# The row maxima of a group: turned by TensorE in float32 and scaled by VectorE, in place of a 16-bit copy and a DMA transpose

## The chip, the cores and the metric

The kernel runs on one core of a Trainium2 chip. The core has TensorE (PE in the profile, its weight loads PEld), VectorE (DVE), ScalarE (ACT), GpSimd (POOL), and SyncE (SP), which here only issues DMAs. Each works through its own queue in the order in which the program stands, and waits on semaphores for the others. Matrix products land in PSUM (8 banks of 2 KB per partition), all else lives in SBUF. The metric is the device time of one execution in microseconds (us); lower is better.

## What is computed

Attention over 8 batches, 12 heads, 448 rows and 64 columns, whose output goes through a layer of 8 experts of 448 tokens each:

```python
q_n, k_n = rmsnorm(q, g_q), rmsnorm(k, g_k)
scores = scale * np.matmul(q_n, k_n.transpose(0, 1, 3, 2))
scores = scores - np.max(scores, axis=-1, keepdims=True)
attn = np.exp(scores)
attn = attn / (np.sum(attn, axis=-1, keepdims=True) + 1e-09)
x = np.matmul(attn, v)            # then [B, H, S, D] -> [B*S, H*D]
logits = x @ w_gate               # pairs in falling order, 448 tokens per expert
out[mask_e] = np.maximum(x[mask_e] @ w1[e], 0) @ w2[e]
```

The change lies in the subtraction of `np.max`. The maximum of a row of scores sits in one partition, while the kernel computes the scores transposed, so it must be carried over to the free axis, as one row of 448 numbers per head.

## The kernel before

**Two stages.** Attention runs from the start to about 430 us, the router and the experts from there to the end. The change lies in the first. Attention works in 24 groups of 4 heads (`g` = 0 to 23); groups 0 and 1 (`EARLY`) have a path of their own, without the transposes below, and 22 groups take the common one.

**One group.** q and k are loaded (`load_qk`, L239 and L231) and normalised (ACT L289, L301, L303, L327; DVE L295; POOL L306 to L309, L330, L359), split into a high and a low half in 16 bits (`hi`, ACT L368; `lo`, POOL L371) and turned by two DMA transposes on SP's queue, `trh` for the high halves and `trl` for the low ones (`transpose`, L380, kq<-s). Then:

- `max_score` (PE L501) multiplies the high halves into a PSUM tile pm, seven blocks to a group; `max_reduce` (DVE L510) takes the maxima of a block into two columns of mx. The pool of pm has one buffer, so a block's products wait until the maxima of the block before are taken.
- `put_max` (ACT L519) scales the 14 columns of maxima into a 16-bit tile qm, `tr_max` (SP L430) turns qm into mt by a DMA transpose of 128x128, and `row_max` (SP L436) moves the 14 rows of mt by a DMA into rowq, whose two rows hold the maxima of the group.
- `scores` (PE L532, 12 products, and L534, 4 products with rowq, which subtract the maximum) fills psc; `exp` (ACT L540) makes e; `split` (POOL L556) makes the low half pl; `av` (PE L582, and L588 to L592) multiplies with v into po; DVE normalises and splits po (L632 to L652) into xa.
- After six pairs of heads a batch is done: SP stores xa (L667, L670) and turns it by four DMA transposes for the gate (`xtr`, L659).

**What sets the order.** `plan` lists every piece of work with its engine, what it needs and which buffers it uses; a table of numbers, `ORDER`, names the sequence in which all pieces are written out, and thereby the order on every engine's queue. Nothing is reordered when the program runs: an instruction that waits holds up all that stand behind it on its engine. On SP, a `tr_max` or `row_max` that waits holds up loads, stores and the transposes of q and k. Buffers: kq 3, s1 2, pm 1, psc 2, po 2, pl 5. `early` (DVE L1183 to L1223) is the router's work on the first 21 columns of logits; it stands among the last groups of attention.

Of the kernel before, what the change touches and what calls it, by code (L numbers as in the profile page):

```python
# [89 lines left out]
class Attention:  # L90
# [420 lines left out]

    def put_max(self, g, a=None):
        scale = 0.125 / (self.QS * self.KS)
        o, i = (t[:, :14].rearrange("p (h b) -> p h b", h=2) for t in (self.qm[g % 2], self.T["mx", g]))
        some = [(slice(0, 128), slice(0, 7))]
        if a is not None:
            some = [(slice(0, 128), slice(4 * a, 3 + 4 * a)), (slice(64 * a, 64 * a + 64), slice(3, 4))]
        for r, b in some:
# [429 lines left out]
    def plan_first(self, plan, g, a):
# [51 lines left out]
        "Cq2FHv3QHwHx3RCvCw2H2I2e3o3n493T3S3U3V373W4dOJCxCy2JOOOROI2f2g3pHy2hH-Cz4AC+3qHz4BI03rOHOMOLOKONC-I24CD0U92i2j"  # L1000
        "3EI3H+3sI13tI4I53uD1OUOSUAD2UBD3D438392n3F3GUC3vI7OQD5D6UD4DI6I84e4E3w3y3AOPOTD7D8UEUFI9IBIAD9UGDAUHOV2kOWOZDB"
        "OdOYObOaDCUIDDDEIC4gOcOXOeUJUKDFULDG4fOhOfOi4F3z3x4G0B4H3B3CDHDIIDIE4I3+3-IGOk3XIH51DJ5Q5S3Y5U5RUMUNDKIJOgDLDM"
        "IMIKIO4JIN4hIP4L4iDNDOOj3a4jUOUPIQDPDQUQURIS3d3ZOlOmDRDSUS3DIFIIIL4MOoOsOtOpOqOr3b53IRIT4k4mDTDUIUOnUTOu4K4l3c"
        "4N3e3f5V5TDVIV52DW404146OwIXDX54DYO+Oz4nIWIY4o4q4r0CIaIbDZDaIdOv55Ie56DbUUUVDcUWIfIhDdDeUXIgIiIjIkOyDfOxO-P0Dg"
        "UYUZUa5759DhDi4p4O42484s4t586I6K47IlIoImIZIc5AInIpDjIr43UbDk4P4Q5W5Y5BIsDlDmUcUh6JUfIu4RP7P3P2Dn5XDoP8P1PEP6P4"
        "P5IqIv5D5E5Z5aDpUrDqIwIxUsUtP9DrDs5b44455v5xUu5w6LIyIzI+Uk5FI-5c5eDtDuUvPAPBPDPCUwDvDwJ3J0Dx5yUxDyUyJ14uJ4PFPG"
        "ItPH5C5d5z5g5+4SUzU+5fJ25hPNPKPIPLPMPJU-6NDzV0D+J6J9J7JA5iD-E0V1POPPE1E2V2JBJCJD4TUiUj4vE3E4JFPQE5PT5G4V4W6M4w"
        "JEJG0qE66O6PV3PUPSPR5j5-61E7E8V4V5JHJI4X5k5l4+V6JKE9EAV7V8UlUmUnJL607AJ5J8634U6264JJJM6QUoUpJQEBJN5HJO7BUe504-"
        "5I7FUd7CUg5JEC6RJR6nPVEDEEUqPcPaPZPYPbPdEFEGPePfPXEJEK656p6S660D0E6T6UJS4xJT4yPWV9VAEHEIJUJVJW67ELVBVCEMVD6oPj"
        "PiPkPhPgJX6WPlPm4zJPPnEN6V6YVE0FVFVG6X6ZVHEO5K5L5m5N5O7D7E5P5nVIVNVP5oVQ68PtPsPoPqPpPrEPEQJYJbJZJcVXJaJd6a6bER"  # L1010
        "Pu6qESJeJh6rJfETEUPvJjEVP+VYVZVaEWVb7GJiJk6sJlJn6c7I6t6uJmJoEXEY7H6vPzPxPwPyVcVdEZEaJpJqJsEbP-Q0Jg0G0H5MQ10I0J"
        "6x7JEc69VeVfJvJtJw6wJr7K7L6zEdEeVgQ5Q3Q7Q4Q2Q6VhViEfEgVjVkVlJyJ+EhVOVRVTVSEiVU5p5qJzJ-VV7f7hQ8QDEjEk7gK2K0ElVW"
        "Em5s5u82838786VM6A6dVJ5t846B6-QBQAQEQ9QCEnQF7MJu6+7OK17iEoJx5r0K6y7NK3QH7j7k7l7PQG6C6D6EEpK4K5K6K7K8K9Eq6F6G6H"
        "VK856k6m7Q6e6f706lVL6gErVmVnVoEsVpQKQLQJKAKB7S7T0LEtEu0M7RQIQNQMVrKCKD7mExVsVqEyVtKFQOQPEvVuEwKEKG88Vv8A7n7oKJ"
        "KH7U7V8w8x8+Ez8B89E+KIKK8C8X8D8ZQUQSQRQTQQQVVwE-VxVyF0VzQYQdQaQZQbQcF1F2V+7172W3W5W4KLKOF3F4QWQXWDWE8aQeQkF5F6"
        "KM8E0NKP7pKR6h7rKSQgQhF7F8KUKW6i7377W679KVKXFBWFFCWGWHQjKNKQ7s6j7qKT8F0OKYF9Ka7t7u8GKZ0P0Q8HFAQiQfWIWJKb748YQl"
        "QmQnQoQqFDWKFEWLKcKd758I8b8cKf8JFFWMFGQpQtQrW7QsWNWOWPKi7WKgKj8yFHFIWQWRW9W8Kl8KKmKnFJKoFKWAQuQy90WB8z8-FLFMW2"
        "7X787cW07d7YKrKp8MKe8d8LKh8NFP91WCFQ9293KqKsQ+QxQvQwQ-QzWSFNWTFOKtKwFR76KkR6R7R5R4R3R28f8e9oW19s9r9pKuKv94957Z"
        "968gKx7a9P9R7bWUFSWVWWFTFU7v7wV-9q7e9t7xKz0RKyK+8h8j8kL0L1FVFWR8RDRBFXFYR1R0REK-WXWYFZFaL2L6FbWZFcWaWbL398R9RC"
        "L47-8l8081FdRAFeL5L7RFRGRH8i97RIRMRJRNWcWdWeWfWgWlFfFgL87yL9LB7zLCFhFi9Q8O0S999A9uWn8U8P8mWi9SRORQRPLEFjFkLFLH"  # L1020
        "RLRKWvFlFmLJRUFnWwWxFo9w9TLILK9CLLLNLMLOFpWyWzFqRTRSRRRVRWW+FrW-X0FsX1LA7+9B0T0ULDLGRcRdRaRbRY9D9U9VFtFuX28Q9E"
        "9FWo9X9WAgLPLSFvRXReRgFw9vLQLRLTLU8n8o8VWmAh8pFxLVFy8R8S8TLWRZX3LY9ZFz9x9y9zF+X4X5LaLZLb0V9YAHAJ9bRjRiF-G0X6Lc"
        "LdLeG1G2X7LfRfAlWk8WRkRh8q8rX8G3WpWqWrX9G4XAXBXCLjG5LgLhWsWtLkG6WuAKAIRlLXRtRpRqRsRrRoG7RuRvRmRnG89dAiG9XDXEGA"
        "XFLmRz9c9a9+8s9-0WLiLlA0Ln9GAmA18tWhGBGCLpLqLrLsALAMA2A4Aj8uWjAk9M9N8vAoGFAnGGXGXHRxRyRwR+GDXIGEXJLtLv9O9H9e9I"
# [1031 lines left out]
```

## Time and profile before

| | us |
|---|---|
| three runs | 929.72, 933.79, 932.5 |
| their median | 932.5 |
| the profiled execution | 933.5 |
| its span in the profile | 931.7 |
| attention, up to the last normalised pair | about 431 |
| router and experts | about 500 |

The profile lists busy time by engine and stretch, the granted clock of TensorE as a share of its full speed (1.00 is 2.4 GHz), what an engine waited for, and a chain of work followed back from the last instruction. A busy PE is not PE at its peak, since the ends of its matmuls are modelled. For SP the rows give the time that issuing a DMA took; the transfer itself lands later.

### The profile page before, as it was taken

The page shows a single profiled execution, that of the slowest core. Times are in us where ns is not written, and L with a number is a line of the kernel's source. Part 1 is how long each engine was busy: PE and PEld are TensorE (multiplying, and loading weights), DVE is VectorE, ACT ScalarE, POOL GpSimd, SP SyncE. Part 2 cuts the span into 40 slices and gives each one's busy share as a digit, 9 for nine tenths or more (in the row PEclk, how much of TensorE's full clock was granted, in tenths as well). Part 3 has the DMA queues.
Part 4 walks back from the last instruction along what each step waited for, and adds up shares of the span by engine and source line. Part 5 has one row for each costly group of instructions (what it writes and reads, how often), then busy time and mean ns, then how long its engine had stood idle before and what let it go on. Part 6 is the DMA issues. An engine that isn't in the chain of part 4 may idle for free.

```text
span 931.7 us, 29734 instructions
## 1 busy us (share of the span) xinstructions
PE 858.7 (92%) x12783; PEld 566.5 (61%) x12784; DVE 681.9 (73%) x1483; ACT 522.0 (56%) x954; POOL 443.2 (48%) x470
## 2 busy tenths in 40 slices
PE   2799998898999899976799999999999999999996
PEld 1476766665677667756456556565565555655873
DVE  7899988786898689676787777776867758239630
ACT  6999998796989788642142434243333424234421
POOL 7899999886989879882101103021112020120101
PEclk9999999998999899998699999999999999999999
DMA  6689999899999987831454829492937749481401
GB/s 178 155 169 177 182 201 197 207 186 208 206 183 197 189 173 138 168 88 62 150 183 148 276 91 270 141 302 98 301 122 234 198 164 292 150 143 44 152 19 43
DMA packets 262009, 158.02 MB, mean 170 GB/s; under 512 B 183028, under 2 KB 248564, under 8 KB 261876
## 3 DMA queue, kind: packets, MB, share of 16 engines
q1 hardware_dynamic: 256434, 133.63, 61.9%
q0 software_dynamic: 4608, 22.02, 7.0%
q8 instruction: 100, 1.64, 0.8%
q10 hardware_dynamic: 834, 0.46, 0.2%
q14 instruction: 33, 0.27, 0.1%
HBM read 94.40 MB, written 22.02 MB: 125 GB/s over the span
## 4 chain that ended last, share of the span: by engine, by line
issue 37%; PE 24%; POOL 13%; ACT 8%; DVE 8%; DMA 7%; SPq 2%; POOLq 0%; ACTq 0%; DVEq 0%
PE ph L1833 6%; DMA kq<-s 5%; PE psc L532 4%; POOL pl L556 3%; PE py L1850 3%; ACT qn L327 3%; ACT e L540 3%; PE po L582 3%; POOL out_dram L1866 3%; POOL rows L1770 3%; DVE mx L510 2%; PE pm L501 2%; POOL s L371 2%; DVE st L295 1%; PE psc L534 1%
## 5 line engine op out<-in xcount | busy, mean ns | idle before, releaser
L510 DVE TENSOR_REDUCE mx<-pm 128x2 f32<-128x896 f32 x162 | 176.3, 1088 | 55.3 <-PE pm L501 52.8
L1833 PE MATMUL ph<-xt,w1h 128*128 128x448 f16 (+2 forms) x708 | 183.5, 343 | 0.4 <-DVE xt L1791 0.3
L1866 POOL DMA_INDIRECT out_dram<-y,idx x32 | 34.1, 1067 | 307.5 <-ACT y L1852 238.2
L540 ACT ACTIVATE e<-psc 128x896 f32<-128x896 f32 x168 | 147.3, 910 | 34.9 <-PE psc L534 34.5
L556 POOL TENSOR_TENSOR pl<-e 128x896 f16<-128x896 f32 x84 | 140.5, 1688 | 18.9 <-ACT e L540 15.3
L532 PE MATMUL psc<-kq 64*64 64x448 f16 x2016 | 130.0, 360 | 4.6 <-ACT e L540 2.4
L1850 PE MATMUL py<-w2h,hh 128*128 128x384 f16 x384 | 125.0, 326 | 0.0
L1850 PE MATMUL py<-w2h,hl 128*128 128x384 f16 x384 | 125.0, 326 | 0.0
L1850 PE MATMUL py<-w2l,hh 128*128 128x384 f16 x384 | 125.0, 326 | 0.0
L1833 PE MATMUL ph<-xt,w1l 128*128 128x448 f16 (+2 forms) x354 | 119.9, 343 | 0.0
L582 PEld LDWEIGHTS po<-v,e 128*64 128x64 f32 x2940 | 94.0, 139 | 22.0 <-issue 20.7
L582 PE MATMUL po<-v,e 128*64 128x65 f32 x2940 | 105.4, 225 | 1.4 <-issue 0.9
L1850 PEld LDWEIGHTS <-hh 128*128 128x128 f16 x768 | 73.6, 97 | 45.6
L1822 ACT ACTIVATE hh<-ph 128x448 f16<-128x448 f32 x56 | 30.4, 543 | 125.0 <-PE ph L1833 121.9
L1833 PEld LDWEIGHTS <-w1h 128*128 128x128 f16 x708 | 64.8, 97 | 52.6 <-issue 1.5
L1852 ACT ACTIVATE y<-py 128x384 f32<-128x384 f32 x48 | 23.5, 489 | 116.1 <-PE py L1850 95.6
L1770 POOL DMA_INDIRECT rows<-xd,idx x32 | 31.5, 983 | 115.2 <-DVE idx L1540 46.8
L501 PE MATMUL pm<-kq 64*64 64x448 f16 x648 | 63.7, 378 | 23.0 <-DMA kq<-s 13.7
L532 PEld LDWEIGHTS <-kq 64*64 64x64 f16 x2016 | 60.8, 109 | 36.3 <-issue 12.3
L327 ACT ACTIVATE qn<-qkraw,st 128x64 f32<-128x64 f32 x308 | 75.8, 340 | 3.3 <-POOL st L309 2.3
L588 PE MATMUL po<-vs,e 128*128 128x65 f16 (+1 forms) x696 | 65.0, 197 | 3.5 <-DVE z L632 3.5
L1637 DVE SCALAR_TENSOR_TENSOR w2l<-stage,w2h 128x768 f16<-128x768 f32 x64 | 60.2, 951 | 8.9 <-ACT w2h L1633 8.8
(293 smaller groups left out, 1887.9 us busy)
## 6 DMA issues: line engine op xcount, KB each, us to landing
stage<-in_moe_w_dram SPq DMA_DIRECT2D x64, 768.0 KB
vraw<-in_v_dram SPq DMA_DIRECT2D x24, 384.0 KB
xd<-xa SPq DMA_DIRECT2D x16, 576.0 KB
qkraw<-in_q_dram SPq DMA_DIRECT2D x11, 768.0 KB
qkraw<-in_k_dram SPq DMA_DIRECT2D x11, 768.0 KB
vraw<-in_v_dram SPq DMA_DIRECT2D x48, 32.0 KB
xd<-xa SPq DMA_DIRECT2D x16, 96.0 KB
qkraw<-in_q_dram SPq DMA_DIRECT2D x22, 64.0 KB
```

Of the source, the lines that this page charges most:

```text
L327: self.nc.scalar.activation(o[:, h, b], x[:, h, b], AF.Copy, scale=self.T["st", g][:, 1, 14 * i + n:14 * i + n + 1])
L501: self.nc.tensor.matmul(o, q[r, mine], k[r, all_], start=True, stop=True)
L510: self.nc.vector.tensor_reduce(m, p[r, :, :448], axis=AX.X, op=OP.max)
L532: mm(o, k[r, mine], q[r, all_], start=i == 0, stop=False)
L540: self.nc.scalar.activation(e, p[:, :, :448], AF.Exp, scale=scale)
L556: eng.tensor_tensor(l, self.T["e", d], self.T["ph", d], op=OP.subtract)
L582: nc.tensor.matmul(out, self.T["e", d][:, h, q0:q0 + m], self.v32[g % 2][:, h, slot], start=begin, stop=end)
L588: nc.tensor.matmul(out, e[:, h, q0:q0 + m], vh, start=begin, stop=False)
L1637: self.later(0.93, lambda w=w: self.nc.vector.scalar_tensor_tensor(l[:, w], v[:, w], self.WS, h[:, w], op0=OP.mult, op1=OP.subtract), k, i)
L1833: nc.tensor.matmul(p, a, b[:, o], start=st, stop=sp)
L1850: nc.tensor.matmul(p, a[:, f, s], b[:, f, o], start=st, stop=sp)
L1866: st = nc.gpsimd.indirect_dma_start(out=self.out, out_offset=bass.IndirectOffsetOnAxis(ap=self.router.idx[k][:n, c:c + 1], axis=0), in_=y[ ...
```

## The change

For the 22 groups of the common path the maxima stay in float32. mx is now two fixed tiles of 128x64 (14 columns used, the rest set to zero once). `turn_max` on PE multiplies each half of mx (64 partitions) with a 64x64 unit matrix in float32 into a tile of the ring pm, which turns it; `top_max` on DVE reads 14 rows of 128 from PSUM, scales them and writes the 16-bit mt of 14x128; `row_max` on SP moves mt as before. `put_max` remains for groups 0 and 1 alone. The unit matrix is written once by ACT. `tr_max` is gone: SP issues 276 DMAs in attention and not 298. ORDER is a new table.

```diff
-        self.qm = tiles(2, [128, 128], F16, "qm")
+        self.qm = tiles(2, [128, 14], F16, "qm")
+        self.mx = tiles(2, [128, 64], F32, "mx")
+        self.unit = c.tile([128, 64], F32, name="unit")
...
-    def tr_max(self, g):
-        t = self.T["mt", g] = self.w.tile([128, 1, 128], F16, name="mt", bufs=self.RINGS["mt"])
-        self.nc.sync.dma_start_transpose(t, self.qm[g % 2])
+    def units_of(self):
+        for r in (slice(0, 64), slice(64, 128)):
+            self.nc.scalar.activation(self.unit[r], self.router.ident[r, r], AF.Copy)
+
+    def turn_max(self, g):
+        p = self.T["tm", g] = self.ps.tile([128, 2, 512], F32, name="pm", bufs=self.RINGS["pm"])
+        for n, r in enumerate((slice(0, 64), slice(64, 128))):
+            self.nc.tensor.matmul(p[:64, n, :64], self.mx[g % 2][r], self.unit[r], start=True, stop=True)
+
+    def top_max(self, g):
+        t = self.T["mt", g] = self.w.tile([14, 128], F16, name="mt", bufs=self.RINGS["mt"])
+        i, scale = self.T.pop(("tm", g))[:14, :, :64], 0.125 / (self.QS * self.KS)
+        self.nc.vector.tensor_scalar(t.rearrange("p (n c) -> p n c", n=2), i, -1.0 / self.ROW,
+                                     math.log(self.PSC) / (scale * self.ROW), op0=OP.mult, op1=OP.add)
...
-        self.nc.sync.dma_start(q[0:128:64].rearrange("p (b c) -> p b c", c=128), t[:14, 0])
+        self.nc.sync.dma_start(q[0:128:64].rearrange("p (b c) -> p b c", c=128), t)
...
-                add("put", "A", US["small"], self.put_max, g, after=[("mx", g), ("c", "qm")], make=("top", g),
-                    opens=[("qm", g)], uses=[("mx", g)])
-                add("trm", "S", US["trm"], self.tr_max, g, after=[("top", g)], make=("mt", g), opens=[("mt", g)],
-                    uses=[("qm", g)], move=(1.5, 0.25))
+                add("tmx", "T", 0.11, self.turn_max, g, after=[("mx", g), "unit"], make=("top", g), uses=[("mx", g)],
+                    holds=[("pm", ("tm", g))], modes=[3] * 2)
+                add("cmx", "D", 0.27, self.top_max, g, after=[("top", g)], make=("mt", g), opens=[("mt", g)],
+                    frees=[("tm", g)])
...
+        add("unit", "A", 0.45, self.units_of, after=[("rc", 2)], make="unit")
...
     ORDER = (
-        "00030507040m0u0x0w08090v0n0106020o100+0z0y0-1113121P141Q15161RZs1719181A1S1T1U1C1t1w1s1u1z1x1v1-2L2o2q2s1E1B1V"
+        "0u0m0407050v0w0x08090y0z0n0+0-03020601000oZs11131P12141Q1516171RZt1S181T1U1V1s1x1u1v1t1z1+1A0A101O0B191C1B1D1E
...
```

Three places show how the queues change; line numbers of the changed kernel are 2 to 13 higher.

SP around the maxima of group 11 and the transposes of q and k of group 13 (rows of kq<-s; xt<-xa are the transposes of a finished batch), before:

```order
L430 DMA_TRANSPOSE mt<-qm_131 128x1x128
L659 DMA_TRANSPOSE xt<-xa 128x12x128 x3
L436 DMA rowq_129<-mt 2x7x128
L277 DMA vraw_132<-in_v_dram 128x4x192
L659 DMA_TRANSPOSE xt<-xa 128x6x128
L231 DMA vraw_132<-in_v_dram 64x2x64
L380 DMA_TRANSPOSE kq<-s_4629 128x14x128 x2
```

and now:

```order
L667 DMA_TRANSPOSE xt<-xa 128x12x128 x2
L449 DMA rowq_129<-mt 2x7x128
L667 DMA_TRANSPOSE xt<-xa 128x12x128
L382 DMA_TRANSPOSE kq<-s_4686 128x14x128
L233 DMA qkraw<-in_k_dram 64x4x64
L667 DMA_TRANSPOSE xt<-xa 128x6x128
```

The transpose of qm is gone, two transposes of the batch and not three stand ahead of the DMA into rowq, and the first transpose of group 13 stands behind one more of the batch and ahead of the fourth, where it stood behind all four and two loads of v.

DVE around the last maxima of group 11 (L510 and L521 take maxima; L295 and L297 are sums of squares of a later group; L442 is `top_max`; mx_4157 and mx_1_133 are group 11's, mx_4566 and mx_0_132 group 12's), before:

```order
L510 TENSOR_REDUCE mx_4157<-pm_4450 128x2
L648 CAST xa_3359<-po_4293 128x7x64
L510 TENSOR_REDUCE mx_4157<-pm_4513 128x2
L652 TENSOR_TENSOR xa_3359<-po_4293,xa_3359 128x7x64
L510 TENSOR_REDUCE mx_4566<-pm_4561 128x2
```

and now:

```order
L521 TENSOR_REDUCE mx_1_133<-pm_4488 128x2
L297 TENSOR_REDUCE st_4218<-sq_1_140 128x14
L442 TENSOR_SCALAR mt_4568<-pm_4565 14x128
L660 TENSOR_TENSOR xa_3423<-po_4249,xa_3423 128x7x64
L521 TENSOR_REDUCE mx_0_132<-pm_4597 128x2
```

Between the last maxima of one group and the first of the next DVE now empties the turned maxima, here behind a sum of squares; on PE one block of scores stands between `turn_max` and the next products into pm.

DVE near the end of attention, with the end of `early` before (L1223) and its first row now (L1192); L760 and L768 empty the gate's products of batch 6, z and po belong to pair 44; before:

```order
L1191 TENSOR_SCALAR keyi_105<-keyi_105 128x21
L1192 CAST key_106<-keyi_105 128x21
L1193 TENSOR_SCALAR key_106<-keyi_105 128x21
L1223 TENSOR_TENSOR cmp_107<-key_106,hit0_80 128x672
L760 TENSOR_TENSOR logits_63<-po_9675,lsc_9822 128x24
L761 TENSOR_TENSOR logits_63<-po_9675,lsc_9822 64x8
L632 TENSOR_SCALAR z_9839<-po_9688 128x7
```

and now:

```order
L768 TENSOR_TENSOR logits<-po,lsc 128x24
L769 TENSOR_TENSOR logits<-po,lsc 64x8
L640 TENSOR_SCALAR z<-po 128x7
L644 TENSOR_TENSOR po<-po,z 128x7x64
L656 CAST xa<-po 128x7x64
L660 TENSOR_TENSOR xa<-po,xa 128x7x64
L1192 TENSOR_REDUCE best<-logits 128x21
```

`early` now stands behind the gate of batch 6 and behind the pair of heads 44, where it stood ahead of both.

## Rows read from the trace of the kernel before

**Rows 1.** Busy time by stretch: us and instructions of each engine, granted clock, DMA share.

```profile
core 0: us, PE busy (x) PEld busy (x) DVE busy (x) ACT busy (x) POOL busy (x), PEclk, DMA share, GB/s
50.00:125.00 75.00, 72.76 (x1713) 53.08 (x1712) 69.51 (x99) 74.18 (x163) 72.34 (x67) 1.00 0.95 172
125.00:375.00 250.00, 230.03 (x5622) 168.54 (x5615) 202.46 (x302) 212.32 (x448) 216.05 (x205) 0.97 0.95 188
...
200.00:225.00 25.00, 20.68 (x461) 13.87 (x456) 16.53 (x26) 18.05 (x36) 23.09 (x22) 0.87 1.01 194
...
432.00:931.00 499.00, 479.87 (x3889) 291.37 (x3889) 332.72 (x958) 166.66 (x210) 69.10 (x104) 0.97 0.57 167
```

**Rows 2.** Chain that ended last, shares of 50 to 432 us by line.

```profile
by line: DMA kq<-s 11.9%; PE psc L532 8.7%; POOL pl L556 7.4%; PE po L582 6.4%; issue 6.3%; ACT qn L327 5.8%; ACT e L540 5.8%; PE pm L501 4.8%; DVE mx L510 3.8%; POOL s L371 3.8%; PE psc L534 2.9%; PE po L588 2.5%; SPq L659 2.2%; POOL qn L3
```

**Rows 3.** Pieces of that chain: start us, us, what.

```profile
93.16 5.86 DMA kq<-s
...
213.95 5.54 DMA kq<-s
...
365.17 6.34 DMA kq<-s
```

**Rows 4.** Timeline of SP: start us, us, line, DMA, tiles, count.

```profile
213.25 0.65 SPq L231 DMA_DIRECT2D vraw<-in_v_dram  x1
213.95 5.09 SPq L380 DMA_TRANSPOSE kq<-s  x2
...
359.41 5.66 SPq L659 DMA_TRANSPOSE xt<-xa  x3
365.17 2.52 SPq L380 DMA_TRANSPOSE kq<-s  x1
```

**Rows 5.** DMA issues by tile: ns min/median/max, first and last start in us.

```profile
L430 SPq DMA_TRANSPOSE mt<-qm x22: 1122/1201/1780, 60.0 to 399.4; - x22
L436 SPq DMA_DIRECT2D rowq<-mt x22: 550/582/803, 64.3 to 401.7; - x22
...
L380 SPq DMA_TRANSPOSE kq<-s x44: 1380/1982/4541, 35.7 to 387.6; - x44
```

**Rows 6.** Who waited for whom: us in total, times, longest.

```profile
SPq L436 <- DMA mt<-qm: 11.0, 12, 3.0
...
PE pm L501 <- DMA kq<-s: 13.7, 9, 4.1
PE pm L501 <- DVE mx L510: 6.6, 7, 3.8
PE psc L534 <- DMA rowq<-mt: 1.5, 4, 0.7
```

**Rows 7.** Groups by form up to 425 us: count, busy us, mean ns, idle before.

```profile
L510 DVE TENSOR_REDUCE mx<-pm 128x2 f32<-128x896 f32 x162 | 176.3, 1088 | 55.3 <-PE pm L501 52.8 <-ACT v L477 1.3
...
L582 PE MATMUL po<-v,e 128*64 128x65 f32 x2940 | 105.4, 225 | 1.4 <-issue 0.9 <-DVE xa L652 0.5
...
L295 DVE TENSOR_REDUCE st<-sq 128x14 f32<-128x910 f32 x44 | 47.7, 1090 | 0.9 <-ACT sq L289 0.8
...
L648 DVE CAST xa<-po 128x448 f16<-128x448 f32 x47 | 29.0, 618 | 0.6
...
L632 DVE TENSOR_SCALAR z<-po 128x7 f32<-128x7 f32 x47 | 7.4, 158 | 11.0 <-PE po L592 9.4 <-PE po L582 1.3
...
L519 ACT ACTIVATE qm<-mx 128x14 f16<-128x14 f32 x22 | 4.6, 208 | 0.4 <-DVE mx L510 0.3
```

**Rows 8.** Timeline of DVE near the end of attention.

```profile
402.21 0.32 DVE L1183 TENSOR_REDUCE best<-logits 128x21 f32<-128x168 f32 x1
...
411.25 0.17 DVE L760 TENSOR_TENSOR logits<-po,lsc 128x24 f32<-128x24 f32 x1
```

**Rows 9.** Timeline of ACT and POOL there; idle time before in brackets.

```profile
415.49 1.73 ACT L540 ACTIVATE e<-psc 128x896 f32<-128x896 f32 x2 [6.32 <-PE psc L534]
...
422.49 3.32 POOL L556 TENSOR_TENSOR pl<-e 128x896 f16<-128x896 f32 x2 [0.98 <-PE po L592]
```

More of the change, by code (lines that the diff above doesn't have):

```diff
@@ L163, in maxima @@
         def maxima():
-            for t in self.qm:
+            for t in self.mx:
                 nc.gpsimd.memset(t, 0.0)
@@ L190, in __init__ @@
         D, G = nc.vector, nc.gpsimd
-        self.later = [("P", 0.3, eps, "eps"), ("P", 0.3, maxima, "qm"), ("P", 0.4, rowk, "rowk")]
+        self.later = [("P", 0.3, eps, "eps"), ("P", 0.3, maxima, "mx"), ("P", 0.4, rowk, "rowk")]
         self.later += [("P", 0.47, lambda t=t: zero(t), ("rowq", i)) for i, t in enumerate(self.rowq)]
@@ L505, in max_reduce, with put_max @@
         g, b = divmod(n, 7)
-        if ("mx", g) not in self.T:
-            self.T["mx", g] = self.w.tile([128, 14], F32, name="mx")
         r = slice(0, 128) if some is None else slice(64 * some, 64 * some + 64)
-        m = self.T["mx", g].rearrange("p (h b) -> p h b", h=2)[r, :, b]
+        m = self.mx[g % 2][:, :14].rearrange("p (h b) -> p h b", h=2)[r, :, b]
         self.nc.vector.tensor_reduce(m, p[r, :, :448], axis=AX.X, op=OP.max)
-    def put_max(self, g, a=None):
+    def put_max(self, g, a):
         scale = 0.125 / (self.QS * self.KS)
[L514 to L518, printed above, removed]
+        o, i = (t[:, :14].rearrange("p (h b) -> p h b", h=2) for t in (self.qm[g], self.mx[g]))
+        for r, b in ((slice(0, 128), slice(4 * a, 3 + 4 * a)), (slice(64 * a, 64 * a + 64), slice(3, 4))):
             self.nc.scalar.activation(o[r, :, b], i[r, :, b], AF.Copy, scale=-1.0 / self.ROW,
@@ L865, in plan @@
                 first = n % 7 == 0
-                add("red", "D", US["reduce"], self.max_reduce, n, some, after=[("pm", n, some)], make=("mx", *x),
+                add("red", "D", US["reduce"], self.max_reduce, n, some, after=[("pm", n, some), ("c", "mx")], make=("mx", *x),
                     opens=[("mx", g)] if first else (), uses=() if first else [("mx", g)], frees=[("m", n, some)])
@@ L986, in plan_first @@
                      frees=[("tf", i, *x)])
-        part("put", "A", 2 * small, self.put_max, *x, after=[("mx", *x), ("c", "qm")], make=("top", *x), opens=[("qm", g)],
+        part("put", "A", 2 * small, self.put_max, *x, after=[("mx", *x)], make=("top", *x), opens=[("qm", g)],
              uses=[("mx", g)], port=False)
@@ L1000 @@
[L1000 to L1024, printed above, removed]
@@ new lines @@
+        "2w2U2T2W3H2x2y2z1d2ACPCQ3J1K2BCVCWCXCYCbCZCaCc1L2Y2CCd292X2+301M1NHh2V272-321iHi3134HkHlCeCj1j2D3K3I2a3L1k3M1p"
+        "3g3h3l1q3j1r3i3k3mCk1lCfCgHnHoCh2ZCi2EHq2FHrCnCo2bClCmOFCrCsHs36CtCuOGHuCpCq2c33353N3PHtHw37CvCw3nHj1oHmHpOHOK"
+        "ONOMCx2GHv3oHx2HOLOJOI3O4Y4Z2l2m2e3R2d3Q493T4d3VCy2fOOOROT2I2J3pU92h2g3q2i3r2j3S3U2n3E4c4a3W3G4b3sCzHyHz4AUAC+"
+        "H-I04BC-UBD0I2D1I3UCD24CI5OSD3D4OUI7D5D6OQOPUE3uI6I83839UDUFD7D8UGIBI9D9DAUHOV2kH+3tI1I43vOXOZ4D3w4E3BDBOdOaOY"
+        "ObOcDCUIDD3y4F3zIAICOWOe4e4H3F3A3+4g3x4G5Q3-4I0CDEOjDFOhOi4fDGDHUJUKDIULIDIGIEIH51DJDKUMOfIJ3X3Y5V3Z5UIKIM4JIN"
@@ new lines @@
+        "IFII3C3d3eIL3DDLUNDMOkIOIPDN52DOOgUO4hISDPDQUPUQIQOlOmDR4L4N5T5R4M3a4iIR4jIT3b53OqOsOtOoOrDSDTURDUUS4k4mIUIVIX"
+        "DVDWOpOuOzDX544K3c4l4o554nDYOxOwOnUT4041UUUVIaIY56IbIW57DZDa4qOyIdDbUWDcIfOvIeIg5S4O425WDdUXDeIhIjDf0DDgIiIk4r"
+        "IZIc59O+O-P0Dh5XDiUYUZ460p483f47IlIoDjP5P7P4P3P6P2P14p4s4tImIpUaDkUbUcDlDmIrIu434PUrUs4Q444V4WUh4RIs4XUkUtP8Dn"
+        "DoPEIwDp5Y5Z585v5B5A5D45InIqIvIx5a5bDqPBPDPADr5wDsUuIyIzI+5xI-5F6I6J6N0E5E5c5eDtDuP9PCDvUvDwUwUxJ0J1J3J4DxDyPF"
+        "PGItPH4uUy0F4vUzPKPJPLPIPM5C5d5g5y5zDzD+J6J75+5fJ2J50G5-J9JAD-U+E0PNJBJCE1E2U-V0V1JDJFE3E4POPPPTE50q5i5j4SJEJG"
@@ new lines @@
+        "4T4U61V2E6V3PRPUPQE7E8PSUi5G4wUj4xV4V5V65kUlUmUnE9EAV7JHJIJKEBJLUoJNEC5HV8JQ5IED6L6K6M6OEEPV0H0I5h5l60JOJRUpUq"
+        "634yJ86264JJUe4+7A7C4-Ug5J7E6P6Q6nJSEFEG6RPcPYPdPaPZPbPXJTPWEJEKV96o6S6T656UJUJV6pJWJX66JM4zJP6VEHPePgPhPiVAEI"
+        "VBELPkPfPjVCEMVDENVEEOVFVGJYJb7B67Uf507DEP6W6XJZEQPlJeJc5mVH5nVIJh5KERESPmPuPnET6qEU5LJf6YJi6a7GPpPsPoPtPqPrUd"
+        "VXEVVYEWJjJlJkJmEXEYVZPyJnEZ68VaVbEa7FVNVQVJ5oVP6cVO5N5PVL5s5O5u5tJaJd0J5MJgP+PxPwPzP-Q0PvQ16r6s6tJo7I6b6Z6u0K"
+        "0L6vEbJpJq7JJsJt7H7K7LQ7Q2Q3Q5VcVdVeEcVf696AVg82856B8387Jv6wJw7fEdQ6Q4EeJyEfVhViVjEgVkJ+JzJ-6x6z7hVRVSVTEhEiVl"
@@ new lines @@
+        "HKYaNCNDNENFBSHNHOYETFTGHLBRNGNJY5NHNIHMHPTKYDTMTLTITJTNHQHRHSNKYFBTYGNPNMNNNQCFHTTHTOTRTUTSYbHUYcYdYeTPTQTTNL"
+        "BUBuYfYgYhBvYiYjYkBWBxByBtY4Y6B+B-C0BwYpYsYoYrYqYnYlNSNTNVHVHWNWNONRCECGTVTbTZTXTaTWTYNYHXHYNbHbHcNZNcNhNeHZYz"
+        "Y+HaY-Z0NUNXNaNfNiTcTgTdThTeTiTfCKZ5Z6HdNkHeZ1Z7HfNlNnNoHgZ8NqNrCHNtCICJNuCLYmZ9YtBzNdNgNjNmTjTpTlTnTkToTmZEYv"
+        "YuYwYxZFYyNzNwNxNpNsNvCMTqTsTvTrTwTuTtZMZGZHZIZrZNZOZPZQN+NyN-O0O1O3O6O2O4O7O5O9OAOCODZ2O8TxTyT-TzU1U0T+OBZAZC"
+        "Z3ZRZTZSOEZVZWZXZYZZU2U4U6U3U7U8U5ZdZeZfZgZhZiZlZ4ZJZKZUZBZDZaZnZbZcZpZoZLZqZmZkZj"
```

38 lines of the change are left out of this document (22 added, 16 removed).

## The prediction

> **What bounds the kernel now.** The busy times by stretch come first, since a sum over the whole span mixes two programs. From 432 us on TensorE is busy 479.87 of 499 us and nothing in that stretch is touched [rows 1]. So a gain of attention moves the end one for one, and the question is what attention waits for. From 50 to 125 us ACT is busy 74.18 of 75 us and POOL 72.34: two engines are full. From 125 to 375 us no engine is: ACT 212.32, POOL 216.05, PE 230.03 of 250, and the granted clock falls to 0.97 [rows 1]. Something that is not an engine holds that stretch up. If it ran as densely as the one before, POOL would need 216.05 x 75 / 72.34 = 224 us of it, ACT 212.32 x 75 / 74.18 = 215 us. So 250 - 224 = 26 us is the most that freeing the hold-up can give.
>
> The chain of waits names it: its largest share in attention is the landing of kq<-s, 11.9% of 382 us, 45 us [rows 2], in nine pieces between 93.16 and 365.17 us [rows 3]. What a piece waited for is to be read on SP's own timeline: the transposes at 213.95 us start 0.05 us after the load before them was issued, and those at 365.17 us 0.10 us after three transposes of xa that took 5.66 us [rows 4]. They were not late for want of data just made; they stood in SP's queue. The transposes of q and k are what PE waits for: 13.7 us directly, against 1.5 us for the row of maxima itself [rows 6]. So the row is hardly late; it is the place that the maxima take on SP that counts.
>
> **The change part by part.** The sum is made on the profiled execution, 933.5 us (span 931.7).
>
> *SP loses 22 transposes.* One costs SP 1.20 us of issuing in the median [rows 5], and the DMA behind it waits for its landing 11.0 us in all, 0.5 us per group, with every load and transpose behind it [rows 6]. That is 1.7 us per group, or 37 us of SP's time. What reaches the end is what the nine pieces give: two come as a pair, so eight times 1.7 = 13.6 us if each is issued that much earlier. The table adds to it at the two places that I looked up: group 13's transpose no longer stands behind a fourth transpose of the batch and two loads, and in the row shown [rows 4] the three transposes ahead of the piece at 365.17 us are no longer ahead of it. Against it, POOL and ACT are the next to be late. Bounds: 0, if SP fills the slots with longer issues of what remains, and -26, POOL's limit above. I take -10, three quarters of the eight, since the stretches between the pieces are led by ACT, POOL and PE already.
>
> On this a page of the Trainium skill speaks otherwise. Here a transpose costs SP 1.20 to 1.98 us in the median and up to 4.54, the plain DMA into rowq 0.58 [rows 5]. "Advanced Engine Details and Errata", section X-Bar Transpose, states that transposes are as fast as ordinary DMAs on trn2. By that rule a slot would be worth 0.58 + 0.5 us and the term about -6; the rows speak against it, and the sum goes by the rows.
>
> *The clock.* A full clock in the 250 us, where it is 0.97 [rows 1], would be worth up to 7.5 us of PE's time, and the one stretch shown at 0.87 is one in which PE was busy 20.68 of 25 us only [rows 1]. I give back a fifth of that, -1.5 (0 to -7.5).
>
> *ACT loses 22 copies* of 0.208 us, 4.6 us [rows 7]. ACT leads at least 11.6% of the chain [rows 2]: -0.5 (0 to -4.6).
>
> *DVE gains 22 instructions* of 14x128 from PSUM; the 14 partitions don't matter if the time goes by elements per partition. Between 128x7 at 158 ns and 128x448 at 618 ns [rows 7] that is 158 + 121 x 1.04 = 284 ns, 6.2 us in all. DVE leads about 4% of the chain by the one line shown [rows 2]; I double it for the lines not shown: +0.4 (0 to +6.2).
>
> *PE gains 44 float32 products* of 64x64. The nearest row is L582, float32 with 65 columns: 105.4 us for 2940, 36 ns each packed, and 225 ns each alone [rows 7]. So 0.07 to 0.45 us per group; I take 0.16, nearer the packed end as two halves of the array work at once: 3.5 us. PE leads at least a quarter of the chain [rows 2]: +0.9 (+0.4 to +9.9).
>
> *A new wait on pm.* pm has one buffer and now serves eight tiles per group, not seven. PE stands at `turn_max` until the last maxima are taken, and then, one block of scores later, at the next products into pm until DVE has emptied the turned tile. Behind PE's wait stand scores and av, so ACT and POOL behind those. In the order of group 11 DVE has a sum of squares between, 1.09 us like a step of maxima [rows 7], about as long as the block of scores on PE covers. Before, PE waited for the maxima 7 times for 6.6 us, 0.94 us each [rows 6]. If one group in three meets such a wait, 7 x 0.94 = 6.6 us, a third of it on the chain: +2 (0 to +6.6).
>
> *The end of attention.* `early` ran from 402.21 to 411.25 us, and only then did DVE empty the gate's tile, which PE needed; ACT then stood idle 6.32 us, and the last splits on POOL began at 422.49 [rows 8, 9]. Now the gate and pair 44 go first, so the scores and their exponentials run during `early`. But the release of pair 45 stands behind it: 9 us from about 413, plus 2 us, is 424.5, against the 425.8 at which POOL ended before (422.49 + 3.32). -1.4 (-3 to +1).
>
> *The start.* The first load of q moves ahead of a gain's load, and the memset that the gains wait for moves to POOL's end; I put it at -0.3 (-1 to +1), an estimate from loads of about 0.6 us on SP.
>
> Sum: 933.5 - 10 - 1.5 - 0.5 + 0.4 + 0.9 + 2 - 1.4 - 0.3 = 923.1. The median of the runs is 1.0 us below the profiled execution, so I say **922**.
>
> **The rivals.**
>
> *Hidden anyway, about 931.* The DMA engines are busy 0.95 of the time in both stretches [rows 1], and SP's issues of kq<-s stretch from 1.38 to 4.54 us [rows 5], as they would if the queues behind them were full. Then the slots that are freed are spent in longer issues. A group turns 28 blocks of q and k, 14 of a batch, and one of maxima, so only a 43rd of the turning goes. Likewise if the wait moves: SP now stands at the DMA into rowq until DVE is done. The SP term is then about -2.5 and the clock's 0: 933.5 - 2.5 - 0.5 + 0.4 + 0.9 + 2 - 1.4 - 0.3 = 932.1, 931 on the median's scale. For it: the DMA share. Against it: plain loads between the transposes take the usual 0.65 us [rows 4], and attention moved 172 GB/s while ACT was full and 188 when it was not [rows 1].
>
> "DMA: Bandwidth & Descriptors", section Rules for kernel authors, of the Trainium skill says to issue a DMA early and wait late, so that its fixed cost overlaps. By that rule the old path was free already, which is this rival: the row cost PE 1.5 us [rows 6], and the trace agrees for the row, while what the rule leaves out is the queue behind it.
>
> *Slower: PE stands for DVE in every group, about 941.* DVE is busy 202.46 of 250 us [rows 1]; if in all 22 groups PE waits one step of maxima or sum of squares longer, 22 x 1.09 = 24 us [rows 7], a third of it reaches the end: +8. With SP's gain eaten: 933.5 - 0.5 + 0.4 + 0.9 + 8 - 0.3 = 942, 941 on the median's scale. With SP's gain gone, and the end's with it, it passes the mark of 0.5% from 0.57 us of new wait per group on: a third of 22 x 0.57 is 4.2, which is what 933.5 + 0.5 lacks to 938.2 on this execution's scale. For it: one buffer, order fixed. Against it: several pieces of PE's work stand ahead of each `turn_max`.
>
> *More than forecast, about 908.* SP was all that held the 250 us up: -26 in place of -11.5 gives 908.6.
>
> **How the numbers follow.** A run of this kernel tells 0.5%, 4.7 us, from no change: 927.8 and 937.2 are the marks. Forecast (914 to 930): 0.52. Hidden: 0.25 (928 to 936). Slower: 0.15 (937 to 946). More: 0.08 (905 to 913). Faster is the forecast but for 0.02, More, and 0.03 of Hidden: 0.61. Slower is that rival without 0.01: 0.14. The same is the rest, 0.25. For 8 in 10 the range leaves out the lower end of More and most of Slower: 908 to 938.
>
> **What would show it.** Right: the landing of kq<-s shrinks from 45 us on the chain, PE's 13.7 us for it falls under 8, ACT's and POOL's busy share rises in the middle stretch and its length falls by some 10 us; `turn_max` packed, `top_max` near 0.28 us. Wrong: issues of kq<-s grow longer and the middle stretch stays at 250 us (Hidden); PE's waits at pm for DVE grow over 20 us (Slower); `early` still followed by an idle ACT (the end's term).

## The result

The changed kernel takes 923.2 us (median of 4 runs, 922.7 to 924.6) against 933.1 us before (929.7 to 935.5): a ratio of 0.9892, 95% interval 0.9869 to 0.9916, or 9.9 us less. The forecast was 922, range 908 to 938. So the total came out as forecast. The experiments show that its largest term did too; several of the small ones were wrong by amounts that cancel, and that part of the agreement is luck.

The profiled execution of after is 924.6 us with a span of 922.8; before, the span was 931.7.

**Where the 9 us are.** Two marks on the timelines, the issue of the last group's DMA into rowq on SP and the first step of the router that has all logits on DVE, cut both executions into three. Before, SP and then DVE (columns: start us, us, engine, line, operation, tiles, count):

```profile
401.68 0.58 SPq L436 DMA_DIRECT2D rowq<-mt  x1
```

```profile
434.08 0.21 DVE L1183 TENSOR_REDUCE best<-logits 128x7 f32<-128x56 f32 x1
```

and after:

```profile
393.54 0.59 SPq L449 DMA_DIRECT2D rowq<-mt  x1
```

```profile
425.57 0.21 DVE L1192 TENSOR_REDUCE best<-logits 128x7 f32<-128x56 f32 x1
```

The last row of maxima leaves 8.1 us sooner. From it to the second mark takes 32.4 us before and 32.0 after, and from there to the end of the span 931.7 - 434.1 = 497.6 and 922.8 - 425.6 = 497.2. So the gain lies ahead of the last group's row; the end of attention gave 0.4 us, and router and experts nothing.

**The middle stretch.** Busy time by stretch in after (columns as in [rows 1]):

```profile
core 0: us, PE busy (x) PEld busy (x) DVE busy (x) ACT busy (x) POOL busy (x), PEclk, DMA share, GB/s
50.00:125.00 75.00, 72.82 (x1717) 53.25 (x1716) 71.04 (x105) 73.22 (x156) 72.43 (x69) 1.00 0.90 170
125.00:375.00 250.00, 232.74 (x5851) 176.40 (x5849) 209.18 (x323) 218.68 (x445) 223.42 (x209) 0.99 1.00 198
```

Against [rows 1] the same 250 us now hold 7.4 us more of POOL's work (223.42 against 216.05) and 6.4 us more of ACT's. At the density of the stretch before, POOL would be full at 72.43 / 75 x 250 = 241 us, so 18 us are still open there.

**Who waits for whom**, in after (columns as in [rows 6]; PEld is the weight load, which meets the wait first):

```profile
PE pm L514 <- DVE mx L521: 4.2, 10, 0.7
...
PE psc L542 <- DMA rowq<-mt: 2.9, 2, 2.1
PE pm L514 <- DMA kq<-s: 2.7, 2, 1.5
...
PE pm L514 <- DVE mt L442: 0.4, 1, 0.4
...
PE pm L437 <- DVE mx L521: 0.2, 1, 0.2
```

```profile
PEld pm L437 <- DVE mx L521: 1.4, 5, 0.6
```

PE's wait for the transposes of q and k falls from 13.7 us in nine pieces [rows 6] to 2.7 in two. The share of their landing on the chain, the other sign that the prediction named, can't be read in after: the chain followed back from its end breaks off at 421 us. Experiment 1 gives it. The waits that the change could bring are small: 0.2 us at the turn (1.4 at its weight loads), 0.4 us at the next product into pm.

**The new instructions** (groups of after up to 425 us), and the DMA issues on SP (ns, least, median, most, as in [rows 5]):

```profile
L437 PE MATMUL pm<-unit,mx 64*64 64x64 f32 x88 | 7.0, 236 | 0.3 <-DVE mx L521 0.2
...
L442 DVE TENSOR_SCALAR mt<-pm 14x128 f16<-14x128 f32 x22 | 5.9, 269 | 3.2 <-PE pm L437 2.8
```

```profile
L382 SPq DMA_TRANSPOSE kq<-s x44: 1387/2322/4897, 35.6 to 389.8; - x44
```

The scaling takes 269 ns against the 284 interpolated; the products are 88 matmuls of 236 ns, packed to 7.0 us, where I had 3.5. The transposes of q and k that are left take SP *longer* to issue than before: 2.32 us in the median against 1.98 [rows 5], and the DMA engines' share in the middle stretch rises from 0.95 to 1.00. That was the mark set for the rival Hidden, and it came true, while Hidden's result did not: SP's time was partly spent in longer issues, and PE's wait for them still fell by 11 us.

### The profile page after: what moved, and what is told of

The parts are those of the page before. It is cut to its first block, busy times and chain, and to the rows that moved or that the text cites. A ratio compares the mean times of both kernels' runs of the same rounds, so it can differ in the third digit from the quotient of the medians.

```text
span 922.8 us, 29897 instructions
## 1 busy us (share of the span) xinstructions
PE 856.5 (93%) x12871; PEld 571.9 (62%) x12872; DVE 683.6 (74%) x1505; ACT 521.0 (56%) x934; POOL 442.9 (48%) x470
## 4 chain that ended last, share of the span: by engine, by line
issue 35%; PE 11%; POOL 5%; DVE 1%; DMA 1%; POOLq 0%; ACT 0%; SPq 0%; DVEq 0%
PE ph L1842 6%; PE py L1859 3%; POOL out_dram L1875 3%; POOL rows L1779 3%; DMA stage<-in_moe_w_dram 1%; DMA rows<-xd,idx 0%; PE rp L1315 0%; POOL spacer L1874 0%; PE rp L1386 0%; DVE or L1290 0%; DVE cmp L1300 0%; PE rp L1543 0%; PE py L1868 0%; PE py L1794 0%; PE psc L692 0%
## 5 line engine op out<-in xcount | busy, mean ns | idle before, releaser
L521 DVE TENSOR_REDUCE mx<-pm 128x2 f32<-128x896 f32 x162 | 176.2, 1088 | 36.3 <-PE pm L514 33.6
```

## The experiments

Each ratio is to runs of the kernel before on the same chip; a ratio times 933 gives the microseconds, which can lie up to about 2 us off the median given beside it. Differences between two kernels are differences of these ratios, and their half-widths are the root of the summed squares.

**1. The 22 transposes left out, nothing else** (order of before, ACT still copies, the rows are not the maxima's):

```diff
-        t = self.T["mt", g] = self.w.tile([128, 1, 128], F16, name="mt", bufs=self.RINGS["mt"])
-        self.nc.sync.dma_start_transpose(t, self.qm[g % 2])
+        self.T["mt", g] = self.qm[g % 2]
```

> The kernel before, in its own order, with the 22 transposes of the maxima left out: the DMA into rowq takes the copied maxima as they stand, unturned, so the rows are not the maxima's. Nothing else is changed; ACT still copies, PE and DVE get no new work. SP theory (the gain is SP's queue, freed of 22 transposes): 933.1 - 10 - 1.5 for the clock = about 921.6 us, and PE's wait for kq<-s falls from 13.7 us to under 8. Hidden theory (the DMA engines are full, freed slots go into longer issues): about 930.6. Order theory (the refined order makes the gain): 932 to 934.

Measured: 922.9 us, ratio 0.9894 (0.9849 to 0.9939): -9.9 us, plus or minus 4.2. PE's waits:

```profile
PE pm L500 <- DMA kq<-s: 7.3, 3, 3.5
```

The chain that ended last, shares of 50 to 425 us by line:

```profile
by line: PE psc L531 8.1%; ACT e L539 7.2%; POOL pl L555 6.7%; DMA kq<-s 6.4%; PE po L581 5.9%; ACT qn L327 5.2%; issue 4.7%; DVE mx L509 4.5%; POOL s L371 4.2%; DMA qkraw<-in_k_dram 3.7%; PE pm L500 3.6%; PE psc L533 2.6%; DMA qkraw<-in_q_
```

The landing of kq<-s falls from nine pieces and 45 us of the chain [rows 2, 3] to four pieces and 6.4% of 375 us, 24 us. So freeing SP of these transposes, with the order untouched and no other engine relieved, gives as much as the whole change. It kills the theory that the refined order makes the gain, and it kills Hidden's -2.5. The mean clock of its profiled execution is 0.973, after's 0.980, at nearly the same time, so no gain from the clock can be seen between the two.

**2. The new mechanism in the old order**, the turn placed halfway on PE between a group's last maxima and the next product into pm:

```diff
-        "0u0m0407050v0w0x08090y0z0n0+0-0302060100
...
+        "00030507040m0u0x0w08090v0n0106020oZs100+0z
...
```

> The changed kernel in the order of before: each turn of maxima and its scaling are put halfway on PE between a group's last maxima and the next product into pm, all else stands as before. SP theory: 933.1 - 10 - 1.5 - 0.5 + 0.4 + 0.9 + 2 = 924.4, up to 928 if part of the SP term needed the new places of the transposes. Order theory: 933 to 936, the mechanism's new work with nothing won. Slower theory (PE stands for DVE in every group): above 937.

Measured: 940.8 us, ratio 1.0090 (1.0054 to 1.0126). That is slower than before, but the trace shows two delays that I had put there myself. ACT copied `unit` ahead of its own loads of k, and waited for those:

```profile
3.57 0.52 ACT L432 ACTIVATE unit<-ident 64x64 f32<-64x64 f16 x2 [1.56 <-DVE ident L1085]
5.09 1.34 ACTq L233 DMA_DIRECT2D qkraw<-in_k_dram  x2
8.45 2.52 ACTq L241 DMA_DIRECT2D qkraw<-in_k_dram  x2
11.07 0.63 ACT L291 ACTIVATE sq<-qkraw 128x512 f32<-128x512 f32 x1 [6.98 <-DMA qkraw<-in_k_dram]
```

Before, the squares start at 5.74 us, here at 11.07. And SP stood 8.0 us at the last group's DMA into rowq, issued at 408.33 us. The profile names the first step of `early` for that wait, and I took it so; DVE's timeline says otherwise:

```profile
408.02 0.28 DVE L442 TENSOR_SCALAR mt<-pm 14x128 f16<-14x128 f32 x1 [4.48 <-PE pm L437]
408.23 0.31 DVE L1192 TENSOR_REDUCE best<-logits 128x21 f32<-128x168 f32 x1
```

The scaling stands ahead of `early`, and DVE itself was idle for 4.48 us until the turn, which PE reached only at 407.64 us, behind 96 products of av and 48 of the gate. It was the turn's late place on PE that held the row up. The run says nothing on the change, but that two copies, 0.52 us together, ahead of an engine's loads put its first squares off by more than 5 us.

**3. The same with both places mended** (`Zs` is the task that makes `unit`, `0-` the last of ACT's loads of k at the start; `CH` and `CI` are the last group's turn and scaling, `Zr` is `early`):

```diff
-        "00030507040m0u0x0w08090v0n0106020oZs100+0z0y0-1113
...
+        "00030507040m0u0x0w08090v0n0106020o100+0z0y0-Zs1113
...
-...TjTnToTlTpTkTmYvYwYuCHCICLYxZr
+...TjTnToCHCITlTpTkTmYvYwYuCLYxZr
...
```

> As the run of the changed kernel in the order of before, with two places mended that were of its own making: the scalar engine's two copies for `unit` stand behind its four loads of k, not ahead of them (they had held the start up by 8.8 us), and the last group's turn and scaling stand ahead of `early` (its DMA into rowq had waited 8.0 us for it). SP theory: 922 to 927, since 940.8 - 8.8 = 932.0 and up to 8 more for the end; the new work on PE and DVE then costs 0 to 4 us over the run with the transposes left out. Order theory, that without the refined order the new work eats the gain: 931 to 934.

Measured: 929.2 us, ratio 0.9948 (0.9925 to 0.9971): -4.9 us. The last row's wait on SP is 4.8 us here; as the diff shows, `early` stood behind the scaling in both runs, and what moved is the turn on PE. Against experiment 1 the new work on PE and DVE costs 5.0 us (plus or minus 4.7) in this order; against after the order is worth 5.2 us (plus or minus 3.1). PE now has the wait that the rival Slower spoke of:

```profile
PE pm L437 <- DVE mx L521: 9.6, 14, 2.0
...
PE pm L514 <- DVE mx L521: 4.9, 5, 3.8
...
PE pm L514 <- DMA kq<-s: 2.6, 2, 2.1
...
PE pm L514 <- DVE mt L442: 2.1, 5, 0.6
```

It stands 9.6 us at the turn, 14 times, and 2.1 us more behind the scaling: 0.53 us per group, just under the 0.57 from which that rival was to decide. In after the same two rows are 0.2 and 0.4 us. The refined order puts scores or av between the last maxima and the turn. What part of the 5.0 us is this wait, and what part DVE's 22 scalings, the run does not tell.

**4. The new order with the old mechanism** (ACT's copy where the turn stands, the DMA transpose where the scaling stands):

```diff
-        "00030507040m0u0x0w08090v0n0106020o100+0z
...
+        "0u0m0407050v0w0x08090y0z0n0+0-0302060100
...
```

> The kernel before in the new order: the 16-bit copy stands where the turn on PE stands, the DMA transpose where the scaling stands. SP theory: only the end's 1.4 us, the start's 0.3 and the two places where kq<-s moved ahead, 933.1 - 1.7 - 1 to 2 = 929 to 931. Order theory: 923 to 925, all of the gain.

Measured: 979.5 us, ratio 1.0488 (1.0435 to 1.0542), 46 us slower than before. All theories missed. SP's waits:

```profile
SPq L430 <- ACT qm L519: 20.6, 4, 7.7
SPq L436 <- DMA mt<-qm: 20.2, 9, 4.4
SPq L430 <- ACT e L540: 16.7, 8, 8.7
```

The new order lets SP come to the maxima as soon as DVE could have scaled them; with the old mechanism SP then stands for ACT's copy, and all loads and transposes behind it stand too. The order is cut for the mechanism and is no gain by itself.

**5 and 6. The slots put back into after**: 22 transposes of a constant tile that nobody waits for, or 22 plain DMAs of the same 32 KB:

```diff
+        x = self.w.tile([128, 1, 128], F16, name="spare", bufs=2)
+        self.nc.sync.dma_start_transpose(x, self.rowk)
```

> The changed kernel with 22 DMA transposes of 128 by 128 in 16 bits put back on SP, one per group where the scaling stands, of a constant tile into a spare one: nobody waits for them, and the DMA into rowq does not wait for their landing. SP theory, slots count: 22 x 1.2 us of slots of the 22 x 1.7 us that were freed, so about 0.7 of the 10 us come back, 929 to 931; if the place in the queue is all, 933. If only the wait for the landing counted: 923 to 925. Hidden theory: 925 to 926.

```diff
+        x = self.w.tile([128, 1, 128], F16, name="spare", bufs=2)
+        self.nc.sync.dma_start(x[:, 0], self.rowk)
```

> The changed kernel with 22 plain DMAs of the same constant tile (128 by 128 in 16 bits, 32 KB) on SP where the other run had 22 transposes; nobody waits for them. SP theory by slots: a plain issue takes 0.58 us, half of the 1.2 of a transpose, so half of the 12.9 us that the transposes cost, 929 to 930. If any place in the queue costs the same: 935 to 936. If the turning is what costs: 923 to 925.

Measured: the transposes 936.2 us, ratio 1.0046 (1.0012 to 1.0081), 14.4 us (plus or minus 3.9) over after; the plain ones 929.2 us, ratio 0.9942 (0.9909 to 0.9974), 4.7 us (plus or minus 3.8) over it. Their issues on SP and their landing, transposes first:

```profile
L445 SPq DMA_TRANSPOSE spare<-rowk x22: 1172/1245/2383, 60.8 to 403.5; - x22
...
DMA to landing us min/median/max: 3.0/4.4/5.3
```

```profile
L445 SPq DMA_DIRECT2D spare<-rowk x22: 513/602/1228, 61.1 to 399.8; - x22
...
DMA to landing us min/median/max: 3.1/5.4/5.4
```

PE's wait for kq<-s goes back to 11.9 us with the transposes and to 4.9 with the plain DMAs, where after had 2.7; first the transposes, then the plain ones:

```profile
PE pm L516 <- DMA kq<-s: 11.9, 8, 2.8
```

```profile
PE pm L516 <- DMA kq<-s: 4.9, 4, 2.2
```

With the transposes put back, the chain (50 to 425 us) shows the landing of kq<-s at 11.0%, 41 us:

```profile
by line: PE psc L542 13.1%; PE po L592 11.1%; DMA kq<-s 11.0%; PE pm L516 6.3%; DVE mx L523 5.3%; POOL pl L566 4.3%; PE psc L544 4.2%; issue 3.7%; PE po L598 3.5%; ACT e L550 3.0%; PE po L602 2.7%; PE po L600 2.6%; ACT qn L329 2.6%; POOL s 
```

So a place in SP's queue has a price with nobody waiting for what stands in it, and the price fits the time that the issue takes: 14.4 us for 22 x 1.245 = 27.4 us of issuing, 4.7 for 22 x 0.602 = 13.2, with some 4 us of doubt on either. The wait for the landing is not needed for it. A rival is that the added transfers burden the DMA engines and not SP's queue. These two runs do not rule it out, since the two kinds of transfer may burden the engines differently; but the chain speaks against it. It has seven landings of kq<-s with the transposes put back, of 5.9 us on average, against four of 6.0 in experiment 1: more of the transposes come late, and on average they are no slower on their way.

The rule that the prediction weighed, of the Trainium skill ("Advanced Engine Details and Errata", section X-Bar Transpose, that a transpose on trn2 is as fast as an ordinary DMA), is borne out here for the landing, as far as the trace tells it (4.4 against 5.4 us in the median, of only 4 of the 22 in either run), and not for the issuing queue (1.245 against 0.602 us).

**7. `early` back at its old place in after:**

```diff
-...NuCLYmZ9YtBzNd...ZGZHZIZrZNZOZP...
+...NuCLYmZ9ZrYtBzNd...ZGZHZIZNZOZP...
```

(Two letters are one task of the table: `Zr` is `early`, `Z9` the last step of pair 43, `ZI` that of pair 44.)

> The changed kernel with `early` at its old place, ahead of the sum of gate 6 and of pair 44 on DVE; nothing else moves. The end's term by my sum: +1.4, up to +3: 924.6 to 926. If `early` made most of the 9 us by which attention ends sooner: above 928. If it is covered: 923.

Measured: 922.5 us, ratio 0.9882 (0.9830 to 0.9935), 0.9 us less than after (plus or minus 5.4). No gain from the move of `early` can be seen: with it back ahead of pair 44, the time from the last row to the router's mark is 423.28 - 392.44 = 30.8 us, against 32.0 in after.

**8 and 9. The products on PE left out**, in the new and in the old order (the scaling takes the unturned maxima from SBUF, so the rows are not the maxima's):

```diff
-            self.nc.tensor.matmul(p[:64, n, :64], self.mx[g % 2][r], self.unit[r], start=True, stop=True)
...
-        i, scale = self.T.pop(("tm", g))[:14, :, :64], 0.125 / (self.QS * self.KS)
+        i, scale = self.mx[g % 2][:14, None, :].to_broadcast([14, 2, 64]), 0.125 / (self.QS * self.KS)
```

> The changed kernel without the 44 float32 products on PE: the scaling on DVE takes its values straight from the unturned maxima, so the rows are not the maxima's, and no tile of pm is taken for the turn. By my sum the products are worth 0.9 us and the new wait on pm 2: 923.2 - 2.9 = 920.3. If the wait is covered: 922 to 923. If PE stood for DVE at a third of 22 steps (Slower): 915.

> The changed kernel in the order of before, as it took 929.2 us, without the 44 products on PE: the scaling takes the unturned maxima, so the rows are not the maxima's, and pm has no tile for the turn. In that order PE stood 9.6 us at the turn for DVE's maxima and 2.1 us at pm for the scaling. Theory of the wait (what the old order loses is PE standing at the turn): the run falls by about 5 us, to 923 to 925, near the 922.9 of the kernel that only leaves the transposes out. Theory of the tail or of DVE's 22 scalings: it stays at 928 to 930.

Measured: 925.4 us, ratio 0.9896 (0.9849 to 0.9943), and 929.0 us, ratio 0.9951 (0.9923 to 0.9980). Neither fell. Read alone that says that turn and wait are free, but the scaling had changed with its source (group of the scaling, up to 425 us):

```profile
L440 DVE TENSOR_SCALAR mt<-mx 14x128 f16<-14x128 f32 x22 | 23.4, 1064 | 0.0
```

That is the new order's kernel: 1064 ns in place of 269, 17.5 us more of DVE in all, and PE stands 10.9 us for DVE's maxima where it stood 4.2:

```profile
PE pm L512 <- DVE mx L519: 10.9, 17, 2.7
```

The stand-in had a price of its own, which hides what was to be measured. Experiment 12 gives that price.

**10. The stores of xa on ACT's queue**, an attempt at a faster kernel:

```diff
-            nc.sync.dma_start(o[:, :, part], x[:, 4 * part:4 * part + 3])
+            (nc.scalar if b < self.B - 1 else nc.sync).dma_start(o[:, :, part], x[:, 4 * part:4 * part + 3])
```

> The changed kernel with 28 of the 32 stores of xa issued by ACT's queue, not SP's, at the same places in the program. SP theory: 28 plain slots off SP are worth what the 22 added plain DMAs cost, 0.27 us each, so -7.6 us; ACT pays 28 x 0.6 = 17 us of its time, and if ACT's time counts at the 0.43 that SP's did, +7: 921 to 925. If SP is no longer what holds attention up: 928 to 932, ACT's price alone.

Measured: 929.1 us, ratio 0.9956 (0.9935 to 0.9977), 6.0 us (plus or minus 3.0) over after. The 28 issues took 17.6 us on ACT's queue, but ACT works on beside most of them, as here:

```profile
132.80 0.59 ACTq L675 DMA_DIRECT2D xd<-xa  x1
...
132.97 0.95 ACT L370 ACTIVATE s<-kn 128x896 f16<-128x896 f32 x1
```

By ACT's timeline 12.5 of the 17.6 us lie beside an activation, so they can't be counted as time that ACT lost. The change makes the kernel slower; by what path is not shown.

**11. The 22 copies put back on ACT:**

```diff
+        x = self.w.tile([128, 14], F16, name="spare", bufs=2)
+        self.nc.scalar.activation(x, self.mx[g % 2][:, :14], AF.Copy, scale=-1.0 / self.ROW,
+                                  bias=math.log(self.PSC) / (0.125 / (self.QS * self.KS) * self.ROW))
```

> The changed kernel with the 22 copies of the maxima put back on ACT, into a tile that nobody reads. By my sum +0.5 us: 923.7. At ACT's full share, 22 x 0.208: 927.8. At the share at which SP's time counted (0.43): 925.2.

Measured: 926.3 us, runs from 922.0 to 932.5, ratio 0.9948 (0.9911 to 0.9984): 5.2 us over after, plus or minus 4.1. The copies take 22 x 0.208 = 4.6 us. So full price cannot be told from a quarter of it; that they are free is unlikely.

**12. A second scaling on DVE behind each first**, from the maxima in SBUF:

```diff
+        x = self.w.tile([14, 128], F16, name="spare", bufs=2)
+        self.nc.vector.tensor_scalar(x.rearrange("p (n c) -> p n c", n=2), self.mx[g % 2][:14, None, :].to_broadcast([14, 2, 64]),
+                                     -1.0 / self.ROW, 1.0, op0=OP.mult, op1=OP.add)
```

> The changed kernel with a second scaling of 14x128 on DVE behind each of the 22, from the maxima into a tile that nobody reads. By my sum +0.4 us: 923.6. At DVE's full share, 22 x 0.28: 929.4. At SP's share: 925.9.

Measured: 931.0 us, ratio 0.9986 (0.9963 to 1.0009), 8.8 us (plus or minus 3.1) over after, above what any theory gave. The groups say why:

```profile
L445 DVE TENSOR_SCALAR spare<-mx 14x128 f16<-14x128 f32 x22 | 22.1, 1006 | 0.0
...
L442 DVE TENSOR_SCALAR mt<-pm 14x128 f16<-14x128 f32 x22 | 5.9, 269 | 2.5 <-PE pm L437 2.2
```

The added work was 22.1 us, not 6. PE's wait for the maxima rises with it, from 4.2 us in after to 11.5:

```profile
PE pm L517 <- DVE mx L524: 11.5, 19, 1.8
```

Taken by its real length, DVE's time costs 8.8 / 22.1 = 0.40 us per us at this place of the order. With that price the stand-in of experiment 8 cost 17.5 x 0.40 = 7.0 us; the run lay 0.4 us over after, so turn and wait together would be worth about 6.6 us in after, and in the old order, by 21.2 - 6.0 = 15.2 us more of DVE at 0.40, less the 0.3 us by which that run lay over experiment 3, about 5.8. Both are estimates with some 5 us of doubt either way.

## Why the prediction was right, step by step

*SP's queue, -10.* Right, and shown: leaving the transposes out, alone, gave 9.9 us, and putting 22 of them back into after took 14.4. The reading of the chain and of SP's timeline [rows 2 to 4] named the cause. I had read two late transposes there. The same timeline has it for all nine that PE waited for: each starts 0.04 to 0.12 us after the end of the issue before it, and SP's issues fill about 300 of the 350 us from 50 to 400. Of the three quarters that I took, nothing more can be said than that they lie well within the interval.

*The price of a slot.* I counted issue and landing alike, 1.2 + 0.5 us. The extra transposes, without a waiter, cost 14.4 us (plus or minus 3.9), no less than the 9.9 (plus or minus 4.2) that the removed ones gave. So the landing is not needed; that the issue time alone carries the price fits the two runs and is not proved by them.

*The clock, -1.5.* Not shown. The granted clock of the middle stretch does rise, from 0.97 [rows 1] to 0.99 in after and 0.98 in experiment 1, but experiment 1 and after take nearly equal times at mean clocks of 0.973 and 0.980. No run changes the clock alone, so the term stays open.

*ACT, -0.5 of 4.6 us.* Too small, as far as the runs go: the copies cost 5.2 us (plus or minus 4.1) when put back. I had taken ACT's share of the chain, 11.6% [rows 2], for the price of its time.

*DVE, +0.4.* The length was right, 269 ns; the price was not. At 0.40 us per us, an estimate from experiment 12, 5.9 us cost 2.4, six times the term. The failed step is the same: a share of the chain that one line leads is not what a microsecond more of that engine costs. DVE is busy 209 of 250 us in after [rows 1 give 202 before], and what is added to it shows up in PE's wait for the maxima, 11.5 us in experiment 12 against 4.2.

*PE, +0.9, and the wait on pm, +2.* The products took 7.0 us, not 3.5: the trace has 88 matmuls for 44 products. The wait that I priced at up to 6.6 us is in the old order, 9.6 + 2.1 us, and is gone in the new, 0.2 + 0.4. Their common price of some 6 us is an estimate only; no run measures it cleanly, and this stays open.

*The order.* I gave it -1.4 at the end and -0.3 at the start, and a part of SP's term. By the marks the end gave 0.4, `early` nothing that can be seen, and the order as a whole 5.2 (plus or minus 3.1). (The sum for the end, as I wrote it, gives 413 + 9 + 2 = 424 and not 424.5.) Part of the end's mechanism did come: ACT's idle time of 6.32 us is gone, and POOL's last splits end 21.1 us behind the last row, at 414.6 us, where they ended 24.1 us behind it before. But what follows them up to the router's mark takes 10.9 us and not 8.3, and nearly all of that is lost again. What I missed is that the new order takes PE's standing at the turn away. I had looked at the order around one turn, group 11's, and made of it that one group in three would wait; in after PE's matmuls stand there once, for 0.2 us.

So the sum of the small terms, -0.4 forecast and -0.2 measured (after against experiment 1, plus or minus 4.8), was right by cancelling, which is luck: the new work costs about 5 us where I had 2.8 with ACT's relief, and the order gives back about 5 where I had 1.7. The rival Slower named a wait that is there in the old order, 11.7 us of it, in the run that lost half of the gain; that the wait is what lost it is likely and not shown, since experiment 9, without the products, was no faster. Hidden had a right sign, the longer issues, and a wrong conclusion.

## What to carry to other kernels

When a queue's issuing engine stands behind itself, price an edit by the issue time that it takes off the queue. In this kernel a third to a half of it reached the end. To test it, put the same slots back with nobody waiting. The share of the chain that an engine leads is no price for its time: here 0.40 us per us for an engine whose one line shown led 3.8%. And look at the duration of the stand-in in an experiment before believing its verdict.
